# The point at which the third and fourth quarter of x are split, in a kernel that mixes attention and a Fourier transform

## Chip, cores and metric

The kernel runs on one core of one Trainium2 chip. The metric is the device time of one execution in microseconds (us), the median of several runs. Before the change it is 1727.48 us (3 runs, 1727.0 to 1727.79).

## What is computed

The input x has 2048 rows of 512 numbers. From it come a gate, an attention with 32 heads, and a Fourier mixing along both axes; all in float32.

```python
g = sigmoid((x * gate_w).sum(-1))
q, k, v = x @ wqkv                      # 32 heads of 16
a = concat(softmax(q @ k.T / 4) @ v) @ wo
b = Cr @ (x @ Wr.T) - Ci @ (x @ Wi.T)   # real part of the two-axis DFT
out = g * a + (1 - g) * b
```

## The kernel before

**Split operands.** TensorE multiplies in a reduced format (fp32r). To keep the accuracy, most operands are split in a rounded part hi and a rest lo, and each product is made three times: hi by hi, hi by lo, lo by hi. `split` (L332) is two instructions: a cast on ScalarE writes hi (L333), a subtraction on VectorE or GpSimd writes lo (L334). Both operands of that subtraction lie in SBUF.

**A product** (`products`, L324, with `halves_of`, L181) is a 128x512 result from a contraction over 512: four parts d of 128 rows, three combinations each, so twelve *pairs* of matmuls. The two matmuls of a pair work on rows 0 to 63 and 64 to 127 and write two PSUM tiles, which are added later. After each pair `beside` (L288) advances a counter, the slot, and `run_due` (L270) emits what `after(n, f)` (L263) has set for that slot. So `after(n, ...)` counts pairs of products ahead, and the place of an instruction in its engine's order follows from it. Nothing is reordered afterwards: each engine goes through its instructions in the order in which they are emitted.

**x** comes in transposed, as four quarters c of 512 columns, each in four parts d. The text calls the split of part d of quarter c (counted from 0) *xc.d*: x2.0 to x2.3 are those of the third quarter, x3.0 to x3.3 those of the fourth. All loads of x and of the weights are issued by SyncE at the start (L541 to L553). The DMAs of SyncE use eight semaphores in turn, so each waits until the one eight places ahead of it has landed.

**The first products** (L582 to L600), with the slot of their first pair:

| name here | slot | product | PSUM |
|---|---|---|---|
| F (`project_first`) | 0 | q, rows f = 0 and 1, quarter 0 | two s tiles |
| P0 | 24 | k, f = 0, quarter 0 | xy, first |
| P1 | 36 | q, f = 0, quarter 1 | xy, second |
| P2 | 48 | k, f = 0, quarter 1 | s |
| P3 | 60 | q, f = 0, quarter 2 | xy, first |
| P4 | 72 | k, f = 0, quarter 2 | s |
| P5 | 84 | q, f = 0, quarter 3 | xy, second |
| gate sums (L573) | 96 | x by the gate's weights, 32 matmuls | s |
| P6 | 96 | k, f = 0, quarter 3 | xy, first |

There are two xy pairs of PSUM banks, taken in turn, so P3 can start only when P0's result has been taken out, and P5 when P1's has. In P6, six pairs after the gate sums, four transposes follow that read zr, a ScalarE copy of the gate sums (L576).

**A take** (`take_t`, L483) brings a product out of PSUM. ScalarE copies one half to tx (L489), VectorE adds the other half to it (s; listed under L278, the line that emits what is due), ScalarE casts the sum to eh, GpSimd subtracts to el, and SyncE stores both to memory (L499). The tile tx has one buffer, so the next copy to tx waits for the sum that reads the last one; eh has three, so the fourth cast to eh waits for the landing of the first one's store. Takes 1 and 2 belong to F, take 3 to P0, take 4 to P1, take 5 to P2, and so on. "Sum", "eh 3" or "el 3" below are the parts of take 3.

Among these VectorE also makes four small copies gw from gc (L549, slot 40), and the splits of the second halves of wq (L564, from slot 84) and wk (L565).

Of the kernel before, what the change touches and what calls it, by code (L numbers as in the profile page):

```python
# [53 lines left out]
def build(tc, xT, wqkv, wo, wrT, wiT, cr, ci, gate, out):  # L54
    nc = tc.nc
    with ExitStack() as ctx:
# [194 lines left out]
        with ExitStack() as pf:  # L251
# [11 lines left out]
            def after(n, f, *args):  # L263

                count[0] += 1
                due.append((slots[0] + n, count[0], f, args))
# [112 lines left out]
            with ExitStack() as px:  # L379
# [182 lines left out]
                for d in range(ND):  # L562
                    after(1 + 2 * d, split_w, wk, d, rk[d], nc.vector, near)
                    after(84 + 5 * d, split_w, wq, d, rq[d], nc.vector, far)  # L564
                    after(130 + 12 * d, split_w, wk, d, rk[d], nc.vector, far)  # L565
                    for c in range(1, NC):
                        after(24 * c - 6 + 4 * d, split_x, d, c)
                def gate_sums():

                    ps = s1()  # L570
                    for d in range(ND):
                        for c in range(NC):
                            nc.tensor.matmul(ps[32 * c:32 * c + 32, 0, :], gw[:, d, 0:32], raws[d][:, q4[c]],  # L573
                                             start=d == 0, stop=d == ND - 1, tile_position=(0, 32 * c))
                    zr = ep.tile([P, 512], F32, tag="el", name="zr", bufs=4)
                    nc.scalar.copy(zr, ps[:, 0, :])  # L576
                    for b in range(4):
                        after(6, nc.tensor.transpose, ps[:, 1, b * P:(b + 1) * P], zr[:, b * P:(b + 1) * P], ident)
                    zt = ps[:, 1, :].rearrange("p (b c k) -> p b c k", b=4, c=NC)[:, :, :, 0]
                    after(7, nc.scalar.copy, z.rearrange("p (c b) -> p b c", b=4), zt)  # L580
# [555 lines left out]
```

## Time and profile before

| | us |
|---|---|
| median of 3 runs | 1727.48 |
| the profiled execution, its own time | 1726.84 |
| its span, first to last instruction | 1725.1 |
| ScalarE's largest group, `eb<-s` (L234), 512 instructions | 574.7 |
| VectorE's largest group, the maxima (L137), 364 instructions | 441.3 |
| TensorE's largest group, `pvb` (L775), 2052 matmuls | 513.0 |

A line of a timeline has the start in us, the duration in us, the engine, the line of the kernel, the operation, what is written and read by name, the shapes, the count of equal instructions merged, and in square brackets how long the engine stood idle before it and what released it. Engines are PE (TensorE; PEld are its weight loads), DVE (VectorE), ACT (ScalarE), POOL (GpSimd) and SP (SyncE); a q behind it means the engine's queue. A chain of waits has start, duration and what the time went to. In the names, b tiles hold split parts of x, w and c tiles those of the weights, and buffer numbers are left out. The instructions of one engine overlap a little: the next may start before the last has ended.

### The profile page before, as it was taken

To read this page: it belongs to the slowest core of one execution; us is meant where nothing else is said; L and a number is where in the kernel's file an instruction comes from. 1 tells how busy PE (TensorE), PEld (TensorE's weight loads), DVE (VectorE), ACT (ScalarE), POOL (GpSimd) and SP (SyncE) were. 2 spreads that over 40 slices of the span, in tenths; PEclk is the share of its full clock that TensorE was granted. 3 is DMA by queue.
4 is the path that set the end of the run, shared out by engine and by line. 5 is a ranking of instruction groups with operands and counts; after the bars stand their busy time and mean duration, and the time that the engine had idled before them with its cause. 6 is when DMAs were issued, how large, how long until landed. Compare 5 with 4: busy or idle time off the path is not lost.

```text
span 1725.1 us, 36085 instructions
## 1 busy us (share of the span) xinstructions
PE 1712.7 (99%) x13680; PEld 1042.0 (60%) x13680; DVE 1089.6 (63%) x2059; ACT 1507.0 (87%) x2489; POOL 649.0 (38%) x770
## 2 busy tenths in 40 slices
PE   9999999999999999999999999999999999999998
PEld 6988888988888885333333333333455555555554
DVE  6898888999999996666666666666512211122333
ACT  6447889888888888999999999999988888888886
POOL 3672436655555762223233242322322322223222
PEclk9999999999999999999999999999999999999999
DMA  7783557533337663233333242351334244254612
GB/s 255 243 285 75 154 160 214 156 112 115 104 112 210 151 136 72 36 74 58 66 59 68 54 82 44 58 105 39 67 79 94 72 110 91 66 149 140 175 36 101
DMA packets 123710, 193.03 MB, mean 112 GB/s; under 512 B 54112, under 2 KB 56656, under 8 KB 116624
## 3 DMA queue, kind: packets, MB, share of 16 engines
q1 hardware_dynamic: 84464, 170.20, 37.3%
q0 software_dynamic: 38496, 19.47, 5.5%
q8 instruction: 107, 1.75, 0.4%
q10 hardware_dynamic: 576, 1.05, 0.2%
q14 instruction: 67, 0.55, 0.1%
HBM read 129.63 MB, written 61.61 MB: 111 GB/s over the span
## 4 chain that ended last, share of the span: by engine, by line
PE 97%; DVE 1%; DMA 1%; ACT 1%; issue 0%; SPq 0%; DVEq 0%; ACTq 0%
PE pvb L775 28%; PE xy L185 26%; PE s L210 19%; PE s L154 10%; PE s L185 9%; PE s L135 5%; DMA q_d<-eh 0%; DMA raws<-wqkv 0%; DVE fold L160 0%; PE s L573 0%; DVE y L873 0%; DVE s L278 0%; ACT b L333 0%; ACT fold L158 0%; DVE mx L137 0%
## 5 line engine op out<-in xcount | busy, mean ns | idle before, releaser
L234 ACT ACTIVATE eb<-s 128x1024 f32<-128x1024 f32 x512 | 574.7, 1122 | 65.5 <-PE s L210 65.5
L242 ACT ACTIVATE e<-s 128x512 f32<-128x512 f32 x1022 | 605.1, 701 | 0.4 <-PE s L210 0.4
L137 DVE TENSOR_REDUCE mx<-s 128x2 f32<-128x1024 f32 x364 | 441.3, 1224 | 187.9 <-PE s L135 186.7
L775 PE MATMUL pvb<-eb,va 128*17 128x512 f32 x2052 | 513.0, 597 | 0.0
L775 PE MATMUL pvb<-e,va 128*17 128x512 f32 x2044 | 512.1, 597 | 0.0
L160 DVE CUSTOM_DVE_ANT_0 fold<-s,fold 128x512 f32<-128x512 f32 x660 | 444.0, 690 | 52.2 <-PE s L154 24.6
L158 ACT ACTIVATE fold<-s 128x512 f32<-128x512 f32 x660 | 390.1, 603 | 73.3 <-PE s L154 51.0
L210 PEld LDWEIGHTS s<-qs,ks 50*128 50x128 f32 x2048 | 213.8, 184 | 355.1 <-ACT eb L234 254.9
L210 PE MATMUL s<-qs,ks 50*128 50x512 f32 x2048 | 420.4, 434 | 0.0
L185 PE MATMUL xy<-b,c 64*128 64x512 f32 x2448 | 397.0, 392 | 0.0
L154 PE MATMUL s<-ks,qs 48*128 48x512 f32 x1320 | 314.4, 405 | 1.5 <-DVE mx L160 1.0
L185 PEld LDWEIGHTS xy<-b,c 64*128 64x128 f32 x2448 | 283.8, 187 | 16.3 <-issue 1.0
L154 PEld LDWEIGHTS s<-ks,qs 48*128 48x128 f32 x1320 | 172.7, 184 | 46.8 <-DVE mx L160 12.9
L794 POOL DMA_DIRECT2D r_d<-lc x31 | 18.1, 583 | 455.7 <-DVE lc L793 455.7
L775 PEld LDWEIGHTS pvb<-eb,va 128*17 128x17 f32 x2052 | 70.6, 96 | 191.5 <-issue 184.2
L135 PE MATMUL s<-ks,qs 48*128 48x512 f32 x728 | 151.1, 394 | 0.7 <-DVE mx L137 0.7
L787 POOL DMA_DIRECT2D lc<-ob x124 | 62.9, 514 | 160.1 <-DVE ob L784 159.7
L185 PE MATMUL xy<-w,b 64*128 64x512 f32 x768 | 115.6, 392 | 0.0
L365 POOL TENSOR_TENSOR c<-craw,c 128x512 fp32r<-128x512 f32 x84 | 109.4, 1303 | 6.7
L185 PE MATMUL s<-b,chi 64*128 64x512 f32 x670 | 105.2, 390 | 0.0
L364 POOL CAST c<-craw 128x512 fp32r<-128x512 f32 x84 | 53.3, 635 | 125.1 <-PE xy L185 120.1
L891 DVE CAST chi<-craw 128x512 fp32r<-128x512 f32 x40 | 19.6, 490 | 111.0 <-PE s L185 99.3
(136 smaller groups left out, 1531.9 us busy)
## 6 DMA issues: line engine op xcount, KB each, us to landing
qs<-q_d SPq DMA_DIRECT2D x66, 256.0 KB
craw<-ci SPq DMA_DIRECT2D x64, 256.0 KB
craw<-cr SPq DMA_DIRECT2D x60, 256.0 KB
ks<-k_d SPq DMA_DIRECT2D x44, 256.0 KB
qs<-q_d SPq DMA_DIRECT2D x66, 128.0 KB
ab_d<-ab SPq DMA_DIRECT2D x32, 256.0 KB
y_d<-y SPq DMA_DIRECT2D x32, 256.0 KB
o_d<-oh POOLq DMA_DIRECT2D x28, 256.0 KB, 13.8
```

Of the source, the lines that this page charges most:

```text
L135: nc.tensor.matmul(ps[:, j, :], qs[b:b + 48, qb * P:(qb + 1) * P], ks[b:b + 48, c * 512:(c + 1) * 512], start=True, stop=True)
L137: nc.vector.tensor_reduce(mx[p][:, :, qb, c], ps, axis=AX.X, op=ALU.max)
L154: nc.tensor.matmul(ps, qs[b:b + 48, qb * P:(qb + 1) * P], ks[b:b + 48, c * 512:(c + 1) * 512], start=True, stop=True)
L158: nc.scalar.activation(fold[j], ps, AF.Relu)
L160: nc.vector.tensor_tensor_reduce(out=fold[j], in0=ps, in1=fold[j], scale=1.0, scalar=-3.0e38, op0=ALU.add, op1=ALU.max, accum_out=mx[p][:, ...
L185: nc.tensor.matmul(ps[j], lhs[r], rhs[r], start=first, stop=last)
L210: nc.tensor.matmul(pss[j], ks[b:b + 50, kb * P:(kb + 1) * P], qs[b:b + 50, q0:q0 + 512], start=True, stop=True)
L234: nc.scalar.activation(e, ps, AF.Exp, scale=SCALE)
L242: nc.scalar.activation(e[j], pss[j], AF.Exp, scale=SCALE)
L365: sub(lo, raw, hi.bitcast(F32))
L775: nc.tensor.matmul(pvb[r:r + VC, :], va[:, kb, 2 * p + j, :], es[c][j], start=kb == 0, stop=kb == NB - 1, tile_position=(0, r))
L787: nc.gpsimd.dma_start(lc[32 * n:32 * n + 32, :], ob[r + DH:r + VC, :].rearrange("p (s e) -> p s e", e=16))
```

## The change

`split_x` (L405) splits one part of a quarter; the loop that sets the splits due is changed in one number. For quarter 1 nothing changes. The splits of quarter 2 fall due at slots 34, 38, 42 and 46 instead of 42, 46, 50 and 54, those of quarter 3 at 58, 62, 66 and 70 instead of 66, 70, 74 and 78. The first pair on quarter 2 is that of slot 60, on quarter 3 that of slot 84.

```diff
                 def split_x(d, c):
                     split(*xs[d, c], raws[d][:, c * 512:(c + 1) * 512], nc.vector)
...
                 for d in range(ND):
                     after(1 + 2 * d, split_w, wk, d, rk[d], nc.vector, near)
                     after(84 + 5 * d, split_w, wq, d, rq[d], nc.vector, far)
                     after(130 + 12 * d, split_w, wk, d, rk[d], nc.vector, far)
                     for c in range(1, NC):
-                        after(24 * c - 6 + 4 * d, split_x, d, c)
+                        after(24 * c - (6 if c == 1 else 14) + 4 * d, split_x, d, c)
```

What this does to the order of the first instructions on the two engines concerned, from the first instruction that differs (takes numbered as above):

```
ScalarE before: eh1 tx3 eh2 x2.0 eh3 x2.1 tx4 x2.2 x2.3 eh4 tx5 x3.0 eh5 x3.1 tx6 x3.2 x3.3 eh6
ScalarE after:  eh1 x2.0 tx3 x2.1 eh2 x2.2 eh3 x2.3 tx4 eh4 x3.0 tx5 x3.1 x3.2 eh5 x3.3 tx6 eh6
VectorE before: x1.3 sum2 gw sum3 x2.0 x2.1 x2.2 sum4 x2.3 sum5 x3.0 x3.1 x3.2 sum6 x3.3
VectorE after:  x1.3 x2.0 sum2 x2.1 gw sum3 x2.2 x2.3 sum4 x3.0 x3.1 sum5 x3.2 x3.3 sum6
```

TensorE, GpSimd and SyncE have the same order in both.

## The prediction

> **What bounds the kernel now.** I read the page first. TensorE is busy for nearly the whole span, and the chain of work that ended last runs over it:
>
> ```profile
> span 1725.1 us, 36085 instructions
> ...
> PE 1712.7 (99%) x13680; PEld 1042.0 (60%) x13680; DVE 1089.6 (63%) x2059; ACT 1507.0 (87%) x2489; POOL 649.0 (38%) x770
> ...
> PE 97%; DVE 1%; DMA 1%; ACT 1%; issue 0%; SPq 0%; DVEq 0%; ACTq 0%
> ```
>
> The order on every engine is fixed, so time lost or won on TensorE near the start reaches the end whole. The change lies there; the timeline of TensorE, 10 to 45 us:
>
> ```profile
> 16.59 2.88 PE L185 MATMUL s<-b,c 64*128 64x512 f32 x24
> 19.31 1.41 PE L185 MATMUL xy<-b,w 64*128 64x512 f32 x8
> 21.46 2.53 PE L185 MATMUL xy<-b,w 64*128 64x512 f32 x16 [0.74 <-DVE b L334]
> 23.82 2.90 PE L185 MATMUL s<-b,c 64*128 64x512 f32 x24
> 26.56 1.07 PE L185 MATMUL xy<-b,w 64*128 64x512 f32 x8
> ...
> 30.63 3.64 PE L573 MATMUL s<-raws,gw 128*32 128x512 f32 x32
> 34.20 1.65 PE L185 MATMUL xy<-b,c 64*128 64x512 f32 x12
> 35.78 0.66 PE L278 MATMUL s<-ident,zr 128*128 128x128 f32 x4
> ```
>
> An undisturbed product takes 2.72 us (P2, 16.59 to 19.31). P3, the first on the third quarter, takes 4.51 (19.31 to 23.82), P5, the first on the fourth, 4.07 (26.56 to 30.63). They lose 1.79 + 1.35 = 3.14 us, waiting for the splits. That is all that earlier splits could win. Why are they late? The chain of waits over 0 to 60 us:
>
> ```profile
> 16.87 6.68 DMA q_d<-eh
> ...
> 28.63 0.68 DVE s L278
> 29.31 0.61 DVE b L334
> ...
> 29.96 0.73 PE xy L185 x4
> ```
>
> The eh tile has three buffers, so ScalarE's fourth eh cast waits until the first one's store, issued at 16.87, has landed at 23.55 (16.87 + 6.68). ScalarE goes in order: what stands behind that cast, all four splits of the fourth quarter, waits with it.
>
> **The change part by part.** Nothing is added or removed: eight splits (one cast on ScalarE, one subtraction on VectorE) move eight pairs forward. The instruction orders of the two programs show the same sequence on TensorE, GpSimd and SyncE, so no DMA is moved. On ScalarE and VectorE the splits of the third quarter (x2.0 to x2.3) now stand among the takes 2 to 4, those of the fourth still behind the fourth eh cast. What matters is what stands behind a moved split. ScalarE, VectorE and GpSimd before (timelines of one engine; the last lines give durations as min/median/max in ns):
>
> ```profile
> 15.22 0.59 ACT L489 COPY tx<-s 128x512 f32<-128x512 f32 x1 [0.78 <-DVE s L278]
> 15.70 0.62 ACT L278 CAST eh<-s 128x512 fp32r<-128x512 f32 x1
> 16.62 0.59 ACT L489 COPY tx<-xy 128x512 f32<-128x512 f32 x1 [0.29 <-DVE s L278]
> 17.10 0.62 ACT L278 CAST eh<-s 128x512 fp32r<-128x512 f32 x1
> 17.62 0.62 ACT L333 CAST b<-raws 128x512 fp32r<-128x512 f32 x1
> ...
> 23.63 0.62 ACT L278 CAST eh<-s 128x512 fp32r<-128x512 f32 x1 [2.35 <-DMA q_d<-eh]
> ...
> 34.41 0.59 ACT L576 COPY zr<-s 128x512 f32<-128x512 f32 x1 [0.43 <-PE s L573]
> ```
>
> ```profile
> 14.42 0.68 DVE L278 TENSOR_TENSOR s<-s,tx 128x512 f32<-128x512 f32 x1
> 15.02 0.68 DVE L334 TENSOR_TENSOR b<-raws,b 128x512 fp32r<-128x512 f32 x1
> 15.84 0.69 DVE L278 TENSOR_TENSOR s<-s,tx 128x512 f32<-128x512 f32 x1
> 16.45 1.55 DVE L278 COPY gw<-gc 128x32 f32<-128x32 f32 x4
> 17.91 0.68 DVE L278 TENSOR_TENSOR s<-xy,tx 128x512 f32<-128x512 f32 x1
> 18.51 2.89 DVE L334 TENSOR_TENSOR b<-raws,b 128x512 fp32r<-128x512 f32 x2
> ...
> 29.23 0.68 DVE L334 TENSOR_TENSOR b<-raws,b 128x512 fp32r<-128x512 f32 x1
> ```
>
> ```profile
> 16.41 2.74 POOL L278 TENSOR_TENSOR el<-s,eh 128x512 fp32r<-128x512 f32 x2 [14.16 <-ACT eh L278]
> 17.80 1.35 POOL L278 TENSOR_TENSOR el<-s,eh 128x512 fp32r<-128x512 f32 x1
> 19.32 1.53 POOL L278 TENSOR_TENSOR el<-s,eh 128x512 fp32r<-128x512 f32 x1 [0.17 <-ACT eh L278]
> 24.33 1.29 POOL L278 TENSOR_TENSOR el<-s,eh 128x512 fp32r<-128x512 f32 x1 [3.48 <-ACT eh L278]
> ```
>
> ```profile
> L334 DVE TENSOR_TENSOR b<-raws,b x8: 676/688/1605, 12.2 to 22.5; 128x512 fp32r<-128x512 f32 x8
> L278 DVE COPY gw<-gc x4: 167/169/1291, 16.4 to 17.8; 128x32 f32<-128x32 f32 x4
> ```
>
> Three things are read here. A cast ends after 0.62 us and the next instruction may start after 0.52; a tx copy takes 0.59 and 0.48, a VectorE operation 0.68 and 0.60. tx has one buffer: the copy at 16.62 follows the sum started at 15.84, so each sum of a take holds up the next tx. And a subtraction of a split that meets a running el on GpSimd stands until that one ends: the two from 18.51 take 2.89 us against 0.69 for one, the longest 1.605, and the first gw copy, met by the el of 16.41, takes 1.291 against 0.169. Such an operation then ends some 0.55 us after the el (its 0.68 less a head start). An el starts 0.08 after its eh ends (17.72 to 17.80) and takes 1.29 undisturbed.
>
> The data are there: SyncE issues the loads of wqkv at 14.47 after waits on x2.0 and x2.1, ones_d after x2.2, the first store after x2.3.
>
> ```profile
> 14.47 1.06 SPq L538 DMA_DIRECT2D raws<-wqkv  x2
> 15.89 0.89 SPq L554 DMA_DIRECT2D ones_d<-ones  x1
> 16.87 0.39 SPq L499 DMA_DIRECT2D q_d<-eh  x1
> ```
>
> Now the new order, step by step, with these durations.
> 1. The cast of x2.0 stands right behind the first eh: 16.22 to 16.84, 1.4 us earlier than its 17.62.
> 2. Its subtraction now stands ahead of take 2's sum. Ready at 16.87, it meets the first el (16.41 to 17.70) and ends at 18.24. The sum, before at 15.84, starts at 18.16 and ends at 18.85; take 3's tx, before at 16.62, at 18.95.
> 3. Behind it on ScalarE: x2.1 at 19.43, eh 2 at 19.95, x2.2 at 20.47. VectorE: x2.1 from 20.08, then the gw copies, ready at 20.68. el 2 is ready at 20.65. If el 2 comes first, the copies stand until 21.95, and take 3's sum, before at 17.91, starts at 22.20 and ends at 22.89.
> 4. That sum frees the PSUM pair of P3. **The new wait**: TensorE, done with P2 at 19.31, begins P3 at 22.9.
> 5. eh 3 at 22.92, x2.3 23.44, tx 23.96; x2.3's subtraction meets el 3 (to 24.92) and ends at 25.48; take 4's sum ends at 26.08, and the fourth eh starts at 26.11, not 23.63. The store has landed by then: the 2.35 us wait for the DMA goes, and VectorE is late in its place.
> 6. From there: x3.0 26.63, tx 27.15, x3.1 27.63, x3.2 28.15. VectorE: x3.0 meets el 4 (26.82 to 28.12), ends 28.67; x3.1 29.28; take 5's sum 29.88. eh 5 29.91, x3.3 30.43 to 31.05; its subtraction meets el 5 (30.62 to 31.92) and ends at 32.47. Before, the same one ended at 29.23 + 0.68 = 29.91, and P5 went on at 29.96: **+2.6 us**.
> 7. The gate sums follow P5, 2.6 us late. The zr copy, before at 34.41 when they were done, now stands on ScalarE behind eh and wq casts that lag further and starts at 37.7; the four transposes that read it start at 38.3, where the same reckoning of the old order has 35.3. That is 0.4 more than the gate sums' delay: **+0.4 us**. Behind them P6 and the next products find sums and splits done.
>
> Sum: +3.0 us. Against the profiled execution's own 1726.84 us (span 1725.1) that is 1729.9; it stands 0.64 under the median, to which I add: 1727.48 + 3.0 = **1730.5 us**. The same reckoning of the old order ends P5's last split at 29.83 and begins the transposes at 35.3, within 0.1 and 0.5 of the trace.
>
> The unknown is step 3, a race of 0.03 us whose outcome no row shows. If VectorE keeps the port for its copies, take 3's sum starts 1.3 us earlier, P5's last subtraction ends at 31.23 and the sum is +1.8: 1729.3. I take the first, since in every row above the operation that was ready first went first. [...]
>
> **The rivals.**
> - *The change does what it says*: P3 and P5 find their splits ready; -3.14, 1724.3 us. Against it: the fourth quarter stands behind the fourth eh in both orders, and that can't start before the landing at 23.55.
> - *Nothing net*: the third quarter comes in time because the collisions with el don't happen as reckoned; then the store's landing decides again. From eh at 23.63: x3.0 24.15, its subtraction behind the el of 24.33 (to 25.62) 26.2, x3.1 26.8, sum 27.4, eh 27.4, x3.3 28.6, subtraction 29.3 alone or 29.9 behind an el. That is -0.6 to 0: 1726.9 to 1727.5.
> - *Slower still, by the clock*: TensorE would stand for 3.6 us, where the longest wait between products above is 0.74 and the granted clock is 1.00 (the third figure from the end in this row of the windows, behind the busy times; the last two are the DMA's):
>
> ```profile
> 19.00:31.00 12.00, 10.39 (x82) 6.56 (x82) 9.31 (x12) 8.22 (x17) 5.23 (x5) 1.00 0.78 284
> ```
>
> If the clock were halved after that gap, P3 at twice its 2.72 us would end at 28.4 instead of 26.2, and TensorE would reach the last split of P5 at 33.4, 0.85 after it is ready; the zr copy then waits for nothing else, and the sum is +3.5: 1731.0 us. Halved through P4 as well, it is +6.2: 1733.7. I take the shorter. It decides from the gap of step 4, and is less likely with the race's other outcome, whose gap is 1.3 us shorter. [...]
>
> **How the numbers follow.** First outcome (+3.0, spread 0.5) 0.47; the race's other outcome (+1.8) 0.25; nothing net 0.12; clock 0.08; more collisions than reckoned (another el of 1.29 us met, +4.3) 0.05; as meant 0.03. A measurement of this kernel can tell about 0.2%, 3.45 us, from no change. Faster by that: 0.03. Slower: clock, more collisions, and 0.09 of the first outcome, 0.22. The rest, 0.75, is within it. The range runs from nothing net, 1727.3, to one more collision, 1731.8, and 0.5 of spread: 1732.3, leaving out about 0.1; the likeliest case's own range is 1730.0 to 1731.0.
>
> **What would show it.** TensorE between 19 and 24 us: one wait of 2.5 to 3.6 us ahead of P3, on a VectorE sum. ScalarE's fourth eh: after 24.8, waiting for VectorE and no longer for a DMA. Take 2's sum near 18.2, with a split's subtraction of 1.3 us or more ahead of it. Gate sums: 32 to 33.3, not 30.63. From 43 us on the timelines should match, shifted. I am wrong if the sum of take 2 stays near 16, if P3 starts at 19.3, or if the shift at 43 us is not the difference in time.

## The result, and the profile after

The changed kernel takes 1729.76 us (median of 22 runs, 1728.81 to 1731.19), the kernel before 1727.18 us (22 runs, 1726.31 to 1728.92). The ratio is 1.0015, with a 95% interval of 1.0009 to 1.0022: 2.6 us slower, a small loss, but clear of noise. The profiled execution took 1729.55 us with a span of 1727.8, 2.7 more than that of before. One of the eleven runs of fourth_only below took 2576.61 us at a mean granted clock of 0.59; its ratio leaves that run out, and without it the median there would be 1727.23 us.

The timeline of TensorE after the change (start in us, duration, what ran, the idle time before it and what ended that):

```profile
16.88 2.88 PE L185 MATMUL s<-b,c 64*128 64x512 f32 x24
23.39 4.28 PE L185 MATMUL xy<-b,w 64*128 64x512 f32 x24 [3.63 <-DVE s L278]
27.37 3.39 PE L185 MATMUL s<-b,c 64*128 64x512 f32 x24
30.59 2.95 PE L185 MATMUL xy<-b,w 64*128 64x512 f32 x24
33.47 3.64 PE L573 MATMUL s<-raws,gw 128*32 128x512 f32 x32
...
38.64 0.66 PE L278 MATMUL s<-ident,zr 128*128 128x128 f32 x4
```

The stalls inside P3, which waited for splits in the kernel before, are gone. In their place TensorE stands for 3.63 us ahead of P3, and what ends that is a sum on VectorE: take 3's, which empties the PSUM pair that P3 writes. The gate sums start at 33.47 instead of 30.63, 2.84 us later, of which 0.44 us were there already at the first sum on VectorE (14.86 instead of 14.42). VectorE, in its timelines (some lines are from windows of 2 us, which merge less):

```profile
14.86 0.69 DVE L278 TENSOR_TENSOR s<-s,tx 128x512 f32<-128x512 f32 x1
15.46 0.68 DVE L334 TENSOR_TENSOR b<-raws,b 128x512 fp32r<-128x512 f32 x1
17.31 1.37 DVE L334 TENSOR_TENSOR b<-raws,b 128x512 fp32r<-128x512 f32 x1 [1.17 <-ACT b L333]
18.61 0.68 DVE L278 TENSOR_TENSOR s<-s,tx 128x512 f32<-128x512 f32 x1
20.53 0.69 DVE L334 TENSOR_TENSOR b<-raws,b 128x512 fp32r<-128x512 f32 x1 [1.25 <-ACT b L333]
21.14 1.25 DVE L278 COPY gw<-gc 128x32 f32<-128x32 f32 x1
22.57 0.68 DVE L278 TENSOR_TENSOR s<-xy,tx 128x512 f32<-128x512 f32 x1
...
31.39 1.36 DVE L334 TENSOR_TENSOR b<-raws,b 128x512 fp32r<-128x512 f32 x1 [0.61 <-ACT b L333]
```

ScalarE and GpSimd beside it, also in timelines:

```profile
16.66 0.62 ACT L333 CAST b<-raws 128x512 fp32r<-128x512 f32 x1
19.40 0.59 ACT L489 COPY tx<-xy 128x512 f32<-128x512 f32 x1 [2.12 <-DVE s L278]
...
26.45 0.62 ACT L278 CAST eh<-s 128x512 fp32r<-128x512 f32 x1 [1.55 <-DVE s L278]
...
37.93 0.59 ACT L576 COPY zr<-s 128x512 f32<-128x512 f32 x1
```

```profile
16.85 1.29 POOL L278 TENSOR_TENSOR el<-s,eh 128x512 fp32r<-128x512 f32 x1 [14.60 <-ACT eh L278]
21.09 1.26 POOL L278 TENSOR_TENSOR el<-s,eh 128x512 fp32r<-128x512 f32 x1 [2.96 <-ACT eh L278]
```

Read the three engines side by side. Sum 2, which ran right behind x1.3's subtraction, now has x2.0's subtraction ahead of it: at 16.14 VectorE stands 1.17 us for x2.0's cast, then that subtraction meets the el of 16.85 and takes 1.37 us instead of 0.68. Sum 2 is at 18.61, ScalarE has waited 2.12 us for it, and the first gw copy at 21.14 meets the el of 21.09 and takes 1.25 us. The fourth eh no longer waits for a DMA but for VectorE, at 26.45 instead of 23.63. The last line of VectorE is x3.3's subtraction; it ends at 32.75.

The granted clock fell as well. Windows of 1 us of the same run (behind the busy times stand the clock, the DMA's share and GB/s):

```profile
23.00:24.00 1.00, 0.61 (x6) 0.62 (x8) 0.84 (x2) 0.72 (x2) 0.02 (x1) 1.00 0.16 59
24.00:25.00 1.00, 1.00 (x12) 0.99 (x10) 0.55 (x1) 0.90 (x2) 1.00 (x1) 0.94 0.29 111
25.00:26.00 1.00, 1.00 (x8) 1.00 (x6) 1.00 (x2) 0.00 (x0) 0.27 (x1) 0.50 1.02 383
...
28.00:29.00 1.00, 1.00 (x10) 1.00 (x9) 1.00 (x2) 1.00 (x3) 0.43 (x1) 0.85 0.62 236
```

At half the clock for 3.4 us (0.12 + 3 + 0.3; the windows left out stand at 0.50) the matmuls would lose 1.7 us, an estimate: P3 takes 4.28 us from first to last, P4 3.39 where 2.88 is usual. Whether that is the loss, or lies beside it, is a question for the experiments.

### The profile page after: what moved, and what is told of

The parts are those of the page before. It is cut to its first block, busy times and chain, and to the rows that moved or that the text cites. A ratio compares the mean times of both kernels' runs of the same rounds, so it can differ in the third digit from the quotient of the medians.

```text
span 1727.8 us, 36086 instructions
## 1 busy us (share of the span) xinstructions
PE 1713.0 (99%) x13680; PEld 1040.7 (60%) x13680; DVE 1090.3 (63%) x2059; ACT 1507.5 (87%) x2489; POOL 648.8 (38%) x770
## 3 DMA queue, kind: packets, MB, share of 16 engines
q8 instruction: 107, 1.75, 0.4%
## 4 chain that ended last, share of the span: by engine, by line
PE 96%; DVE 2%; DMA 1%; ACT 1%; issue 0%; SPq 0%; DVEq 0%; ACTq 0%
PE pvb L775 28%; PE xy L185 25%; PE s L210 19%; PE s L185 9%; PE s L154 9%; PE s L135 5%; DVE fold L160 1%; DMA raws<-wqkv 0%; DMA q_d<-eh 0%; ACT fold L158 0%; PE s L573 0%; DVE y L873 0%; ACT b L333 0%; SPq L543 0%; DVE mx L160 0%
## 5 line engine op out<-in xcount | busy, mean ns | idle before, releaser
L154 PE MATMUL s<-ks,qs 48*128 48x512 f32 x1320 | 313.3, 405 | 1.6 <-DVE mx L160 1.0
L135 PE MATMUL s<-ks,qs 48*128 48x512 f32 x728 | 147.2, 394 | 0.7 <-DVE mx L137 0.7
```

The source lines that it names most:

```text
L135: nc.tensor.matmul(ps[:, j, :], qs[b:b + 48, qb * P:(qb + 1) * P], ks[b:b + 48, c * 512:(c + 1) * 512], start=True, stop=True)
L154: nc.tensor.matmul(ps, qs[b:b + 48, qb * P:(qb + 1) * P], ks[b:b + 48, c * 512:(c + 1) * 512], start=True, stop=True)
```

## The experiments

The theory: the loss comes from the order. On VectorE the moved subtractions stand ahead of the sums of takes 2 and 3, wait there for casts and for GpSimd, and P3 waits for its PSUM; everything is late up to P5's last split, which decides when the gate sums start. The rivals: the clock is the loss; the fourth quarter's splits crowd ScalarE; TensorE or the loads are full in any order.

The start of the first work differs by some tenths between executions, so the table gives beside the medians two starts less that of sum 1, the first sum on VectorE, which all kernels share: that of the fourth eh and that of the gate sums. They are from the one profiled execution of each kernel. Eleven runs of each experiment; the kernel before ran beside them, 33 runs for each four kernels (1726.84 and 1726.78 us).

| kernel | median us | against before | ratio, 95% interval | fourth eh less sum 1, us | gate sums less sum 1, us |
|---|---|---|---|---|---|
| before | 1727.18 | | | 23.63 - 14.42 = 9.21 | 30.63 - 14.42 = 16.21 |
| changed | 1729.76 | +2.58 | 1.0009 to 1.0022 | 26.45 - 14.86 = 11.59 | 33.47 - 14.86 = 18.61 |
| third_only | 1729.31 | +2.47 | 1.0005 to 1.0023 | 25.98 - 14.39 = 11.59 | 32.98 - 14.39 = 18.59 |
| fourth_only | 1727.27 | +0.43 | 0.9991 to 1.0009 | 23.25 - 14.47 = 8.78 | 30.29 - 14.47 = 15.82 |
| after_p2_twice | 1729.50 | +2.66 | 1.0008 to 1.0026 | 25.57 - 13.95 = 11.62 | 32.60 - 13.95 = 18.65 |
| after_gw | 1728.65 | +1.81 | 1.0001 to 1.0018 | 24.88 - 14.48 = 10.40 | 31.90 - 14.48 = 17.42 |
| after_sub_pool | 1727.80 | +1.02 | 0.9996 to 1.0013 | 23.29 - 14.40 = 8.89 | 31.80 - 14.40 = 17.40 |
| before_p2_twice | 1727.25 | +0.47 | 0.9994 to 1.0012 | 23.88 - 14.47 = 9.41 | 30.86 - 14.47 = 16.39 |
| before_eh6 | 1724.85 | -1.93 | 0.9981 to 0.9998 | 22.53 - 14.31 = 8.22 | 29.52 - 14.31 = 15.21 |
| placed | 1723.76 | -3.02 | 0.9975 to 0.9992 | 23.70 - 14.34 = 9.36 | 27.46 - 14.34 = 13.12 |

What is lost or won up to the gate sums reaches the end: from their start to the end of the span 1693.8 to 1694.6 us pass in all ten profiled executions.

### Each quarter alone: third_only, fourth_only

Both are shown against the changed kernel.

```diff
-                        after(24 * c - (6 if c == 1 else 14) + 4 * d, split_x, d, c)
+                        after(24 * c - (14 if c == 2 else 6) + 4 * d, split_x, d, c)   # third_only
+                        after(24 * c - (14 if c == 3 else 6) + 4 * d, split_x, d, c)   # fourth_only
```

> The changed kernel with only the third quarter's splits moved; the fourth quarter's stay due 6 to 18 pairs ahead. Theory (order: the moved subtractions stand ahead of the sums of takes 2 and 3, so P3 waits for its PSUM pair): nearly the whole loss, +2.5 us against the kernel before, P3 starting 3.6 us late, one gap over 3.4 us and the clock at 0.5 behind it. Rival (the fourth quarter's splits crowd ScalarE): +0.5 or less, P3 at its old place.

> Only the fourth quarter's splits moved. Theory: they stay behind the fourth eh cast, which waits for the first store's landing, so 0 to +0.5 us, P3 and P4 unchanged, P5's last subtraction within 0.2 us of the kernel before. Rival (the fourth quarter's splits crowd ScalarE): +2 us or more. If earlier splits did help here: -1.35 us, P5 without a stall.

The third quarter's move is nearly the whole loss, +2.47 of +2.58; the fourth's alone is within noise (+0.43, and the gate sums 0.4 earlier after sum 1). TensorE's timeline of third_only has the gap ahead of P3, and that of fourth_only has P3 in its old place, its last lines the end of P5; the third view is ScalarE's timeline of fourth_only, with the fourth eh:

```profile
22.93 4.41 PE L185 MATMUL xy<-b,w 64*128 64x512 f32 x24 [2.61 <-DVE s L278]
```

```profile
20.22 1.07 PE L185 MATMUL xy<-b,w 64*128 64x512 f32 x8
21.51 2.54 PE L185 MATMUL xy<-b,w 64*128 64x512 f32 x16 [0.22 <-DVE b L334]
...
29.63 0.73 PE L185 MATMUL xy<-b,w 64*128 64x512 f32 x4 [0.55 <-DVE b L334]
30.29 3.64 PE L573 MATMUL s<-raws,gw 128*32 128x512 f32 x32
```

```profile
23.25 0.62 ACT L278 CAST eh<-s 128x512 fp32r<-128x512 f32 x1 [1.91 <-DVE b L334]
```

In fourth_only P5 still waits for its last split (0.55 us at 29.63): sooner due, but behind the same eh cast, it comes hardly sooner. It ends at 29.58, 0.38 us earlier after sum 1 than in the kernel before, where within 0.2 was expected; the fourth eh started 0.43 earlier there. The profile puts that start down to VectorE, which ended x2.3's subtraction at 23.25, and not to the DMA; so this run shows that the splits stand behind the fourth eh, but not what the eh waits for. One expectation for third_only missed: its gap was not over 3.4 us but 2.61, since P2 began later in that execution (17.42, not 16.88, while sum 1 came earlier); the clock fell to 0.50 there too, in the windows from 25 to 27 us.

### Is it the clock? after_p2_twice

```diff
                 for n, (w, dst, f, c) in enumerate(order):
                     lead = s1() if n in (2, 4) else None
+                    if n == 2:
+                        for d in range(ND):
+                            for i, (h, l) in enumerate(((0, 0), (0, 1), (1, 0))):
+                                halves_of((lead[:, 0, :], lead[:, 1, :]), w[h][d][:, 0:P], xs[d, c][l],
+                                          d == 0 and i == 0, d == ND - 1 and i == 2)
                     project_t(w, dst, f, c, lead and (lead[:, 0, :], lead[:, 1, :]))
```

> The changed kernel with the twelve pairs of P2 issued twice (the second time they start the sum anew, so the result is the same; 2.72 us more work on TensorE, in its gap ahead of P3; the slots don't count them). The gap falls from 3.6 to about 0.9 us and the clock stays at 1.00. Theory (P5's last split decides, the slow clock is covered but for about 0.25 us): within 0.3 us of the changed kernel, +2.3 to +2.6 us against the kernel before, P3 from its start to its end 3.0 us instead of 4.0. Rival (the halved clock is the loss): 1.7 us less than the changed kernel, +0.9 us against before.

TensorE's timeline of it, and a window with the clock:

```profile
16.58 5.60 PE L185 MATMUL s<-b,c 64*128 64x512 f32 x48
22.50 3.22 PE L185 MATMUL xy<-b,w 64*128 64x512 f32 x24 [0.33 <-DVE s L278]
...
31.93 0.73 PE L185 MATMUL xy<-b,w 64*128 64x512 f32 x4 [0.89 <-DVE b L334]
32.60 3.64 PE L573 MATMUL s<-raws,gw 128*32 128x512 f32 x32
```

```profile
24.00:29.00 5.00, 5.00 (x46) 4.18 (x44) 3.79 (x5) 2.68 (x6) 1.68 (x2) 1.00 0.65 246
```

The clock stays at 1.00, and all eleven executions have a mean granted clock of 0.999, where those of the changed kernel have 0.997 or 0.998. P3 takes 3.2 us, and nothing is won: +2.66 us, the gate sums 18.65 after sum 1 as against 18.61. TensorE reaches P5's last split sooner and then stands for 0.89 us. So the loss is there without the slow clock: in the profiled execution of the changed kernel it ran in time that TensorE would have waited.

The same doubling in the kernel before:

> The kernel before with the twelve pairs of P2 issued twice: 2.72 us more work on TensorE, same result. Theory (P5's last subtraction decides when the gate sums begin, in the kernel before too): P3 starts 2.7 us late, its stall falls from 1.8 to 0, P5 ends where it did; within 0.3 us of the kernel before. Rival (TensorE is the bound here): +2.7 us.

```profile
16.75 5.60 PE L185 MATMUL s<-b,c 64*128 64x512 f32 x48
22.19 2.88 PE L185 MATMUL xy<-b,w 64*128 64x512 f32 x24
24.91 2.88 PE L185 MATMUL s<-b,c 64*128 64x512 f32 x24
27.63 3.30 PE L185 MATMUL xy<-b,w 64*128 64x512 f32 x24
30.86 3.64 PE L573 MATMUL s<-raws,gw 128*32 128x512 f32 x32
```

2.72 us more work cost at most some tenths (+0.47, interval across zero; 0.18 at the gate sums). P3's stalls vanish and the time is the same: they were no loss by themselves, since P5's last split came when it came. A visible wait of the busiest engine need not be on the path, if a later one ends at a fixed point.

### What holds the sums: after_gw, after_sub_pool

```diff
-                    after(40, nc.vector.tensor_copy, gw[:, d, 0:32], gc[:, d:d + 1].to_broadcast([P, 32]))
+                    after(26, nc.vector.tensor_copy, gw[:, d, 0:32], gc[:, d:d + 1].to_broadcast([P, 32]))   # after_gw
```

> The changed kernel with the four small gw copies due at slot 26 instead of 40, before GpSimd's first el, so that they meet none. Theory (the copies meet el 2 and hold take 3's sum by 1.5 us): take 3's sum 1.5 us earlier, the gap ahead of P3 2.1 us instead of 3.6 and the clock at 1.00, P5's last subtraction 1.2 us earlier; +1.4 to +1.8 us against the kernel before, 1.0 less than the changed kernel. Rival (the copies cost only their own 0.2 us): P3 within 0.3 us of the changed kernel's, +2.5 us.

```diff
-                    split(*xs[d, c], raws[d][:, c * 512:(c + 1) * 512], nc.vector)
+                    split(*xs[d, c], raws[d][:, c * 512:(c + 1) * 512], nc.gpsimd if c == 2 else nc.vector)   # after_sub_pool
```

> The changed kernel with the subtractions of the third quarter's four splits on GpSimd instead of VectorE; the casts stay where the change put them. Theory (the subtractions on VectorE ahead of the sums open the gap): sums of takes 2 and 3 within 0.2 us of the kernel before (near 15.8 and 17.4), P3 starts at 19.3 without a gap and then waits for subtractions on GpSimd (1.3 us each and in turn with the el), P3 ends 1.3 us late; +1.6 to +2.0 us against before. Rival (the casts on ScalarE ahead of tx and eh open the gap): take 3's sum 1.5 us or more late, P3 2 us late or more.

VectorE's timeline of after_gw, where sum 3 follows x2.1's subtraction at once, and that of after_sub_pool, where sums 2 and 3 are near their old places:

```profile
20.16 0.69 DVE L334 TENSOR_TENSOR b<-raws,b 128x512 fp32r<-128x512 f32 x1 [1.25 <-ACT b L333]
20.77 0.68 DVE L278 TENSOR_TENSOR s<-xy,tx 128x512 f32<-128x512 f32 x1
```

```profile
15.82 0.69 DVE L278 TENSOR_TENSOR s<-s,tx 128x512 f32<-128x512 f32 x1
16.43 0.43 DVE L278 COPY gw<-gc 128x32 f32<-128x32 f32 x4
17.34 0.69 DVE L278 TENSOR_TENSOR s<-xy,tx 128x512 f32<-128x512 f32 x1 [0.49 <-ACT tx L489]
```

In after_gw sum 3 comes 6.29 us after sum 1 (20.77 - 14.48) instead of 7.71, the gap ahead of P3 falls to 1.75 us, the clock stays at 1.00 in the profiled execution, and 1.2 us of the 2.4 at the gate sums are given back (0.8 by the medians, whose intervals are wide enough for both). Half of the delay there was four copies of 0.17 us, the first of which met an el. In after_sub_pool the casts on ScalarE stand where the change put them, and yet sums 2 and 3 are in time and P3 starts without a gap: it was the subtractions on VectorE. Of the loss at the gate sums 1.2 us are left. P3 waits for GpSimd, where the splits' subtractions of 1.3 us and the el now take turns (1.50 us at the longest), but that isn't what decides: TensorE stands again in P5, 0.89 us for x3.3. The els of takes 3 and 4 come late behind the splits, and x3.0 and x3.1 on VectorE meet both (timelines of GpSimd and VectorE):

```profile
24.34 3.03 POOL L278 TENSOR_TENSOR el<-s,eh 128x512 fp32r<-128x512 f32 x2
24.47 3.45 DVE L334 TENSOR_TENSOR b<-raws,b 128x512 fp32r<-128x512 f32 x2 [3.28 <-ACT b L333]
```

In the changed kernel the same two subtractions take 1.96 us. The median, +1.02, lies under the expected +1.6 to +2.0, and its interval includes zero.

### Undoing what binds: before_eh6, placed

```diff
+                took = []
+
                 def take_t(dst, f, c, ps):
...
-                    hi = ep.tile([P, 512], F32R, tag="eh", name="eh", bufs=3)
+                    hi = (rp.tile([P, 512], F32R, tag="raw", name="eh") if len(took) < 3 else
+                          ep.tile([P, 512], F32R, tag="eh", name="eh", bufs=3))
+                    took.append(hi)
```

> The kernel before with three more buffers for the eh of takes 1 to 3, taken from a pool that stands unused then, so that the fourth eh cast doesn't wait for the landing of the first one's store. Theory (that wait holds the fourth quarter's splits in the old order): the fourth eh 0.8 us earlier, when take 4's sum is done, P5's last subtraction and the gate sums 0.8 us earlier, -0.8 us against the kernel before. Rival (the store's landing is not what holds them): 0 within 0.3.

ScalarE's fourth eh now waits for the sum alone, and the fourth quarter follows:

```profile
22.53 0.62 ACT L278 CAST eh<-s 128x512 fp32r<-128x512 f32 x1 [1.35 <-DVE s L278]
```

The gate sums come 1.0 us sooner after sum 1, near the 0.8 expected. The median is lower by 1.93 us; its interval (-3.3 to -0.3) holds both, and where the rest would come from isn't shown.

The two columns of the table, side by side, show what the time hangs on. In eight of the ten kernels the gate sums begin 6.98 to 7.04 us after the fourth eh, whatever TensorE did in between; of the 2.40 us that the change costs there, 2.38 are the fourth eh's delay. The late sums delay that cast, and with it the fourth quarter's splits. The wait of 3.63 us ahead of P3 lies beside this path: from 23.39, at the usual 2.72 us a product, P3 to P5 would end at 31.55 (an estimate), and the gate sums start at 33.47. The two exceptions fit: in after_sub_pool (8.51 us) the splits behind the fourth eh meet one el more, and in the next kernel, placed (3.76 us), their casts no longer stand behind it.

Last, casts and subtractions set each by itself in the kernel before: no subtraction ahead of a sum that could go, all casts ahead of the fourth eh.

```diff
-                    for c in range(1, NC):
-                        after(24 * c - 6 + 4 * d, split_x, d, c)
+                    after(18 + 4 * d, split_x, d, 1)
+                CASTS, SUBS = (32, 32, 38, 41, 42, 46, 47, 50), (37, 38, 43, 44, 45, 54, 55, 66)
+                for n in range(2 * ND):
+                    c, d = 2 + n // ND, n % ND
+                    (hi, lo), raw = xs[d, c], raws[d][:, q4[c]]
+                    after(CASTS[n], nc.scalar.copy, hi, raw)
+                    after(SUBS[n], nc.vector.tensor_sub, lo, raw, hi.bitcast(F32))
```

The gw copies are due at slot 26, as in after_gw.

> The kernel before with each cast and each subtraction of the eight splits placed by itself: no subtraction ahead of a sum that could go, all casts of the fourth quarter but none of the sums ahead of the fourth eh cast, the gw copies due at slot 26. Theory (not the distance but what stands behind a split decides): P3 and P5 without stalls, gate sums 2.8 us earlier than in the kernel before, -2.7 us against it, some 5 us less than the changed kernel. Rival (TensorE can't go sooner because the loads or the ports are full in any order): within 0.5 us of the kernel before.

```profile
16.48 2.90 PE L185 MATMUL s<-b,c 64*128 64x512 f32 x24
19.20 2.90 PE L185 MATMUL xy<-b,w 64*128 64x512 f32 x24
21.92 2.90 PE L185 MATMUL s<-b,c 64*128 64x512 f32 x24
24.64 2.90 PE L185 MATMUL xy<-b,w 64*128 64x512 f32 x24
27.46 3.64 PE L578 MATMUL s<-raws,gw 128*32 128x512 f32 x32
```

P2 to P5 follow each other every 2.72 us. The kernel is 3.0 us faster than the one before and 6 faster than the changed one, with casts up to 20 pairs sooner than in the latter (x3.3 at slot 50, not 70). Splits far ahead were not the mistake, then; standing in front of the sums was. Casts, subtractions and gw copies are all moved here; what each gives isn't shown.

## Why the prediction was right

The direction, the place and the mechanism were right, and the time, 1729.76, lies 0.7 under the 1730.5 forecast: inside the range, and 0.24 under the likeliest case's own, 1730.0 to 1731.0. Of the 0.7, 0.3 is the kernel before, whose median went from 1727.48 to 1727.18 with more runs, and 0.4 is step 7. In the profiled execution sum 1 starts 0.44 us later than in that of before (14.86, 14.42); with that added to the forecast times:

| step | forecast + 0.44 | measured |
|---|---|---|
| 1, x2.0's cast | 16.66 | 16.66 |
| 2, x2.0's subtraction ends; sum 2; tx 3 | 18.68; 18.60; 19.39 | 18.68; 18.61; 19.40 |
| 3, sum 3 | 22.64 | 22.57 |
| 4, P3 starts | 23.34 | 23.39 |
| 5, fourth eh | 26.55 | 26.45 |
| 6, x3.3's subtraction ends | 32.91 | 32.75 |
| 7, transposes later than the gate sums by | 0.4 more | 0.0 more |

The signs named came too, the gap (3.63, not 2.5 to 3.6) and the gate sums (33.47, or 33.03 without the 0.44, for 32 to 33.3) at the edge. Past 43 us the traces match, shifted: the first matmuls of L135 start at 57.61 and 60.46, 2.85 us apart, and the spans differ by 2.7.

**Step 4, the new wait,** came as forecast, but the sum of +2.6 doesn't need it: it runs over the fourth eh and x3.3 (steps 5 and 6), and after_p2_twice shows that more work in that wait changes nothing.

**The race of step 3** went the way that I took. The el started at 21.09, the copy 0.05 us later, and the copy stood: it took 1.25 us, where the median of the four is 0.17. A margin of 0.05 us, forecast as 0.03, is thin, and the forecast had the right side by an argument that no earlier row showed at such a margin; but it went the same way in third_only and after_p2_twice, where the four copies took 1.51 and 1.54 us, against 0.43 in after_sub_pool, where they were through before GpSimd began. That the two engines compete for a port, as the prediction has it, is not shown; the rows show that one stood while the other ran.

**Step 7 failed.** I put 0.4 us on the zr copy. It did start late, at 37.93, and ended at 38.52, but TensorE came to the transposes only then: they start 5.17 us after the gate sums (33.47 to 38.64), 5.15 before (30.63 to 35.78). The step reckoned the old transposes at 35.3, where the old trace has 35.78. 2.6 us after 35.78 is 38.4, later than the 38.3 at which the copy was reckoned to be through: the copy was covered. Without that term the forecast is +2.6, and +2.58 was measured; that the two are so near is luck, since the measured loss has an interval of +1.6 to +3.8 us and can't tell +2.6 from +3.0. The trace can.

**The rival on the clock** had 0.08 and came true in its first half: each of the 22 executions of the changed kernel has a mean granted clock of 0.997 or 0.998, where 65 of the 66 of the kernel before that ran beside the experiments have 0.999. That the clock would be halved was an assumption: in the kernel before no window from 0 to 100 us shows it under 1.00. The changed kernel shows 0.50 from 25 to 28 us. The price was wrong for the profiled execution. I let P3 and then P5 be late by it (+0.5 beyond the forecast); the fall came 1.5 us after P3 began and lasted 3.4, and after_p2_twice, without it, is as slow. One end stays open: the eight executions at 0.997 have a median of 1730.48 us, the fourteen at 0.998 one of 1729.57, and no trace of one at 0.997 was kept. Whether a longer fall costs something there isn't shown.

**The other rivals** fell as reckoned. The change did nothing of what it says for the fourth quarter (fourth_only), for the reason given, the place behind the fourth eh cast. That this cast waits for a store in the old order is shown by before_eh6. The statement that 3.14 us is all that earlier splits could win fits placed: 3.09 at the gate sums.

## What to carry to other kernels

Before moving an instruction forward on an engine that goes in order, list what will then stand behind it and whether that could have gone at once: here two subtractions that had to wait held back sums that were ready, and with them a PSUM pair and, what counted, the fourth eh and all splits behind it. Moving a cast and moving the subtraction that needs it are two decisions, one for each engine. To find out whether a stall of the busiest engine counts, give it more work there: 2.72 us of doubled matmuls cost next to nothing in both kernels.

## What was not expected of the hardware

The clock fell after a gap of 2.61 us too (third_only); in the profiled execution of after_gw, with a gap of 1.75, it stayed at 1.00 (0 to 34 us). Nine of the eleven executions of after_gw have a mean granted clock of 0.998, though, and only two 0.999. A fall to half for 3.4 us would take 0.001 off the mean (1.7 of 1727, an estimate), so the clock probably fell in those nine as well; how long their gaps were isn't on record. In third_only, too, the fall came after the matmuls had gone on, in the window from 24 to 25 us:

```profile
24.00:25.00 1.00, 1.00 (x9) 0.93 (x7) 1.00 (x1) 0.44 (x1) 0.80 (x1) 0.61 0.74 281
25.00:26.00 1.00, 1.00 (x8) 0.93 (x6) 0.95 (x2) 0.02 (x1) 0.00 (x0) 0.50 0.99 371
26.00:27.00 1.00, 1.00 (x7) 0.93 (x6) 0.00 (x0) 1.00 (x3) 0.32 (x1) 0.50 0.37 143
27.00:28.00 1.00, 1.00 (x8) 0.93 (x7) 0.81 (x2) 0.69 (x3) 0.96 (x1) 0.68 0.54 207
```

By these windows the slow stretch of third_only is 3.4 us (0.78 + 2 + 0.64, an estimate), as long as that of the changed kernel, behind 2.61 us without a matmul instead of 3.63. From which gap on the clock falls, and what sets the length of the slow stretch, these runs don't tell.
